# The recurrence's first chunk is started ahead of the solve, chunks 4 to 7 are prepared further back, and five buffers get other places

## The chip, the cores and the metric

One of the eight cores of a Trainium2 chip runs the whole program. The metric is the device time of one execution in microseconds (us). Engines: PE multiplies matrices, PEld loads its weights, ACT, DVE and POOL work element by element, SP issues DMA transfers.

## The reference, cut to what matters

A linear-attention recurrence over 768 steps for 4 x 8 heads of width 40 gives 3072 tokens of width 320; two feed-forward blocks follow.

```python
for t in range(S):                                   # S = 768
    y[:, :, t] = einsum('bhd,bhde->bhe', rt, state)
    Sa = einsum('bhde,bhe->bhd', state, at)
    state = state * wt[..., None, :] - einsum('bhd,bhe->bhde', Sa, bt) + einsum('bhd,bhe->bhde', vt, kt)
x = y.transpose(0, 2, 1, 3).reshape(B * S, H * D)
a, b = x @ w1, x @ w2
x = (a * b @ w3) @ w_out                             # 320 -> 1024 -> 1024 -> 320
h = maximum(x @ w_in, 0.0)
out = h * h @ w_out2                                 # 320 -> 2048 -> 320
```

The weights of the blocks come as 64-bit numbers.

## The kernel before

The recurrence goes by 24 chunks of 32 steps. Within a chunk it is a triangular system, and a chunk is worked off in stages, in this order: `do_x0` (right side of the system: 32 small products of `XL` with `RX`, the state), `do_sa` (times the inverse `TT`), `do_sat` (four transposes of the result `SA`, with copies by ACT into `vs` and `YI`), `do_l` (products of `vs` and `RT`, masked by DVE into `YI`, line 797), from chunk 1 on `do_z` (the old state transposed into `YR`), and `do_ys` (32 products; DVE makes the new state `RX` of them, line 828, and the output `yst`, line 832). The next chunk's `do_x0` needs that state.

Before a chunk can run it is prepared: `prep` loads its image `im` and decays `iw`, scans them on DVE (lines 570 to 580) and multiplies the image (chunks 0 to 3 on DVE, later ones on POOL, lines 592 and 598); `prep_pq` (written pq) makes 32 products, copied by ACT (`Pn`, line 615) and transposed by DVE (`qt`, line 618); `prep_kb` (kb) makes eight transposes of `im`, copied by ACT into `kn` (line 634). Each stores its result to DRAM through SP's queue, and the chunk's loads (`load_x` for `XL`, `load_rv` for `vs` and `RT`, `load_y`) read it back. `solve` inverts the systems of four chunks at once on DVE (lines 665 to 687: `PT` in, steps on `T`, `tt` out); for chunks 0 to 3 it does two halves, and `corner` joins them with two rounds of products on PE (lines 706 and 709).

Between the stages PE works from a list `fill`: first 64 `step`s that fold w3 and w_out into one matrix (line 472, written pw; in the trace two matmuls each), for which ACT (lines 332 to 335) and DVE (line 337) decode 64-bit weights in `raw` and `early` buffers into `wst`; then the token tiles of the first block (`ab`, line 380). The gaps after the stages say how much is pulled.

The order on PE is the order of the code; the other engines' and SP's orders come from a scheduler with priorities. Every engine and SP's queue work strictly in order. SP has at most eight transfers under way: each waits for the eighth before it. Products of the attention go through two PSUM buffers, `pat`, in turn: each stage waits until the one two places before it has been read out. Most other tiles have one buffer, too (`im` and `iw` for chunks 4 and 6 on, `suf`, `kn`, `qt`).

Of the kernel before, what the change touches and what calls it, by code (L numbers as in the profile page):

```python
# [17 lines left out]
C = 32  # L18
# [13 lines left out]
    ("solve", 0), ("kb", 1), ("kb", 2), ("kb", 3), ("prep", 4), ("pq", 4), ("kb", 4),  # L32
)
BETWEEN = {
    (0, "start"): (("prep", 5), ("prep", 6)),
    (0, "x0"): (("corner", 0),),
    (0, "sat"): (("w3",), ("corner", 1, 0)),
    (0, "l"): (("pq", 5), ("corner", 1, 1)),
    (0, "ys"): (("kb", 5), ("pq", 6), ("kb", 6)),
    (1, "start"): (("prep", 7),),  # L40
    (1, "sat"): (("corner", 2, 0),),
    (1, "l"): (("corner", 2, 1),),
    (1, "ys"): (("pq", 7), ("kb", 7), ("solve", 1)),
    (2, "start"): (("prep", 8),),
# [201 lines left out]
def body(tc, img, rv, rd, vn, vp, raw, w1, w2, w3t, wo, win, wo2, ident, maskt, out, dbg=None):  # L246
# [4 lines left out]
    with (  # L251
# [12 lines left out]
        with right, tc.manual_schedule(engines={mybir.EngineType.PE}):  # L264
# [240 lines left out]
            with (  # L505
# [61 lines left out]
                def prep_scan(c):  # L567
                    w_ = pr["w", c][0:104]
                    suf = first(c, "suf", [128, 529], {1: (at, "wt"), 3: (at, "wt")})
                    dve.tensor_tensor_scan(  # L570
                        out=suf[0:104, ::-1], data0=w_[:, ::-1], data1=mark[0:104, ::-1],
                        initial=0.0, op0=ALU.mult, op1=ALU.add)
                    whole = suf[0:104, 1::33]
                    g = gc[0:104, c % 8]

                    dve.scalar_tensor_tensor(out=g, in0=whole[:, 0:16], scalar=LEAST ** C, in1=whole[:, 0:16],
                                             op0=ALU.is_lt, op1=ALU.max)
                    dve.reciprocal(out=inv[0:104, ::33], in_=g)
# [23 lines left out]
                def prep_pq(c, cc):  # L602
# [11 lines left out]
                    qt = first(c, "qt", [128, 2, HZ, C], {1: (at, "yst"), 3: (at, "yst"), 6: (ma, "xr")})  # L614
# [8 lines left out]
                def prep_kb(c):  # L623
# [3 lines left out]
                    kn = first(c, "kn", [128, 2, HZ, 2, D], {1: (at, "rt"), 3: (at, "vs"), 6: (wa, "w1r")})  # L627
# [158 lines left out]
                def do_l(c):  # L786
# [98 lines left out]
                run(OPENING)  # L885
                solved = marks[0]
                YI = at.tile([128, NU, 72], F32, name="YI")
                RT = at.tile([128, 2, 16, C], F32, name="RT", tag="rt")
                XL = at.tile([128, 2, 16, C], F32, name="XL", tag="XL")
                for t in (XL[32:64], XL[96:128], YI[32:64], SA, RT):  # L890
                    nc.any.memset(t, 0.0)
                dve.tensor_copy(out=YI[0:D, :, C:72], in_=idt[0:D, 0:D].unsqueeze(1).to_broadcast([D, NU, D]))
                with tc.issue_after(ld.ins):
                    folds, more_w3 = fold(solved)
                    stage(load_x, 0)
                    stage(load_rv, 0)
                    stage(load_y, 0)
                fill.push(*folds)

                for c in range(NCH):  # L900
# [8 lines left out]
                    stage(do_x0, c, gap=gaps[0])  # L909
# [250 lines left out]
```

## Time and profile before

| | |
|---|---|
| median of 3 runs | 1065.53 us (1065.2 to 1065.82) |
| the profiled execution, its own time | 1073.37 us |
| its span, first to last instruction | 1071.6 us |
| PE busy | 920.5 us (86% of the span) |
| DVE busy | 693.1 us (65%) |
| ACT busy | 475.1 us (44%) |
| POOL busy | 224.0 us (21%) |

Shares of the whole span mix stages with different limits: PE is busy in 38 of the first 100 us and in 92.5 of the 104 us from 195.7 on.

### The profile page before, as it was taken

The numbers are of one execution on the slowest core, as the hardware profiler recorded it, in microseconds if no ns is written. First come the engines' busy times: TensorE is split into PE (matmuls) and PEld (weight loads), VectorE is DVE, ScalarE is ACT, GpSimd is POOL, SyncE is SP. The second block draws the span as 40 slices with busy tenths as digits, with TensorE's granted clock in tenths as the row PEclk, the third lists the DMA queues.
The fourth block names the chain that finished last, engine by engine and source line by source line (L and its number), as shares of the span: only waits on it lengthen the run. The fifth ranks groups of instructions, "written<-read, shape, count | busy, mean of one in ns | idle before, by whom it ended". The sixth has DMA issues, their size and how long they took to land.

```text
span 1071.6 us, 29226 instructions
## 1 busy us (share of the span) xinstructions
PE 920.5 (86%) x12240; PEld 824.2 (77%) x12240; DVE 693.1 (65%) x1366; ACT 475.1 (44%) x975; POOL 224.0 (21%) x304
## 2 busy tenths in 40 slices
PE   1337676899989889879899989889999999999997
PEld 1235554788879788778898889868998898898986
DVE  8753689568966985897489344887456554444432
ACT  2755776443343334433343433775333333333332
POOL 0332025433334443323200000552000000000000
PEclk9999787899999999989899989989999999999999
DMA  8977775676567667666645532665122121000001
GB/s 239 301 221 224 204 204 150 169 182 161 147 153 184 159 153 183 169 155 159 162 118 113 127 94 62 171 184 113 30 62 54 57 49 25 1 25 1 19 7 27
DMA packets 209389, 134.44 MB, mean 125 GB/s; under 512 B 143793, under 2 KB 184114, under 8 KB 209252
## 3 DMA queue, kind: packets, MB, share of 16 engines
q1 hardware_dynamic: 201892, 110.61, 40.6%
q0 software_dynamic: 7072, 21.57, 7.2%
q8 instruction: 98, 1.61, 0.7%
q10 hardware_dynamic: 288, 0.33, 0.1%
q14 instruction: 39, 0.32, 0.1%
HBM read 99.27 MB, written 33.19 MB: 124 GB/s over the span
## 4 chain that ended last, share of the span: by engine, by line
PE 52%; DVE 22%; DMA 12%; ACT 7%; issue 4%; SPq 2%; POOL 1%; ACTq 0%; DVEq 0%; POOLq 0%
PE ph L380 16%; PE po L1020 16%; PE ab L380 8%; PE px L438 4%; DVE T L675 3%; DVE tmp L672 3%; DMA im<-img 2%; PE pat L820 2%; DVE RX L828 2%; DMA early<-w 2%; DVE yst L832 2%; PE pat L792 2%; DVE suf L570 1%; DVE gl L418 1%; DVE wst L337 1%
## 5 line engine op out<-in xcount | busy, mean ns | idle before, releaser
L1020 PE MATMUL po<-wul,rh 128*128 128x320 f32 x384 | 118.3, 308 | 0.0
L1020 PE MATMUL po<-wuh,rh 128*128 128x320 f32 x384 | 118.0, 308 | 0.0
L1020 PE MATMUL po<-wuh,rl 128*128 128x320 f32 x384 | 116.9, 308 | 0.8 <-DVE rl L1007 0.8
L417 ACT CAST gh<-g 128x256 fp32r<-128x256 f32 x96 | 38.9, 405 | 99.2 <-DVE g L412 86.2
L380 PE MATMUL ph<-xh,wih 128*128 128x512 f32 x192 | 76.0, 396 | 0.7 <-POOL wil L351 0.7
L380 PE MATMUL ph<-xh,wil 128*128 128x512 f32 x192 | 75.7, 394 | 0.0
L380 PE MATMUL ph<-xl,wih 128*128 128x512 f32 x192 | 75.6, 394 | 0.0
L820 PE MATMUL pat<-YI,YR 128*40 128x72 f32 (+1 forms) x1536 | 60.8, 244 | 17.0 <-DVE qt L618 15.2
L1020 PEld LDWEIGHTS po<-wul,rh 128*128 128x128 f32 x384 | 72.0, 188 | 4.2
L411 ACT COPY a_sb<-ab 128x256 f32<-128x256 f32 x96 | 35.6, 371 | 89.1 <-PE ab L380 88.6
L1020 PEld LDWEIGHTS po<-wuh,rh 128*128 128x128 f32 x384 | 72.0, 188 | 3.8
L820 PEld LDWEIGHTS pat<-YI,YR 128*40 128x40 f32 x1536 | 55.9, 130 | 22.6 <-DVE qt L618 17.1
L1020 PEld LDWEIGHTS po<-wuh,rl 128*128 128x128 f32 x384 | 71.6, 188 | 1.3 <-DVE rl L1007 1.3
L438 PE MATMUL px<-wph,gh 128*128 128x320 f32 x192 | 66.6, 347 | 6.0 <-ACT gh L417 3.7
L675 DVE TENSOR_TENSOR T<-T,tmp 128x31 f32<-128x31 f32 (+20 forms) x170 | 66.2, 389 | 3.3
L672 DVE TENSOR_TENSOR tmp<-PT,T 128x31 f32<-128x31 f32 (+20 forms) x170 | 63.7, 375 | 3.6
L418 DVE TENSOR_TENSOR gl<-g,gh 128x256 fp32r<-128x256 f32 x96 | 45.9, 478 | 29.7 <-ACT gh L417 29.4
L438 PE MATMUL px<-wph,gl 128*128 128x320 f32 x192 | 61.5, 320 | 3.4 <-DVE gl L418 3.3
L380 PE MATMUL ab<-xh,w1h 128*128 128x256 f32 x192 | 58.0, 302 | 7.4 <-issue 4.0
L438 PE MATMUL px<-wpl,gh 128*128 128x320 f32 x192 | 61.0, 318 | 0.0
L412 DVE TENSOR_TENSOR g<-a_sb,ab 128x256 f32<-128x256 f32 x96 | 40.0, 416 | 31.2 <-ACT a_sb L411 30.2
L380 PE MATMUL ph<-xq,wir 128*128 128x512 f32 x192 | 60.1, 394 | 0.0
(539 smaller groups left out, 2482.5 us busy)
## 6 DMA issues: line engine op xcount, KB each, us to landing
raw<-w3t SPq DMA_DIRECT2D x16, 512.0 KB
YR<-KB_d SPq DMA_DIRECT2D x48, 160.0 KB
im<-img POOLq DMA_DIRECT2D x28, 240.0 KB, 5.0
wt<-AW_d SPq DMA_DIRECT2D x24, 214.5 KB
raw<-wo SPq DMA_DIRECT2D x16, 320.0 KB
RX<-vp SPq DMA_DIRECT2D x24, 208.0 KB
vs<-rv SPq DMA_DIRECT2D x24, 208.0 KB
KB_d<-kn POOLq DMA_DIRECT2D x14, 320.0 KB, 5.6
```

What stands on the lines that cost most here:

```text
L380: mm(out=ps, lhsT=seq[i][0], rhs=seq[i][1], start=(i == 0), stop=(i == 7))
L411: act.copy(out=a_sb, in_=ps[:, 0])
L412: dve.tensor_tensor(out=g, in0=a_sb, in1=ps[:, 1], op=ALU.mult)
L417: act.copy(out=t["gh"][:, ff], in_=g)
L418: dve.tensor_tensor(out=t["gl"][:, ff], in0=g, in1=t["gh"][:, ff], op=ALU.subtract)
L438: mm(out=ps, lhsT=a_, rhs=b_, start=(k == 0 and i == 0), stop=(k == 7 and i == 2))
L672: dve.tensor_tensor(out=tv, in0=Pv[:, :, s, s + 1:n].unsqueeze(3).to_broadcast(sh), in1=Tv[:, :, s, 0:s + 1].unsqueeze(2).to_broadcast(sh) ...
L675: return dve.tensor_tensor(out=o, in0=o, in1=tv, op=ALU.subtract).ins
L792: mm(out=ps[q:q + 64, 0, 32 * i - q // 2:32 * i - q // 2 + 64], lhsT=vs[0:104, i], rhs=RT[0:104, :, i], start=True, stop=True, tile_positi ...
L820: mm(out=ps[64 * y:64 * y + D, b, 72 * z:72 * z + n], lhsT=YR[:, u], rhs=YI[:, u, 0:n], start=True, stop=True, tile_position=(0, 64 * y))
L828: dve.tensor_tensor(out=o, in0=v[r, :, :, C:72], in1=decay.unsqueeze(3).to_broadcast([D, 2, HZ, D]), op=ALU.mult)
L1020: mm(out=po[j][g], lhsT=a_, rhs=b_, start=(ff == 0 and i == 0), stop=(ff == 15 and i == 2))
```

## The change

`do_x0` of chunk 0 and its loads stand behind the opening's last pq, ahead of the solve and of the kb of chunks 1 to 3; the rest of the opening becomes `SECOND_PART`. Pq and kb of chunks 4 to 7 stand further back among the stages. `wi` and `qt` of chunk 3, `kn` of chunks 1 and 4 and the small `x1` of `corner` get other places, away from those of `XL`, `yst`, `RT`, the common `kn` and `x2`. DVE's decode of later weights is ordered behind `do_l` of chunk 0 (`hold`). No operation is added or removed.

```diff
 OPENING = (
     ("prep", 0), ("prep", 1), ("prep", 2), ("prep", 3), ("pq", 0), ("kb", 0), ("pq", 1), ("pq", 2), ("pq", 3),
-    ("solve", 0), ("kb", 1), ("kb", 2), ("kb", 3), ("prep", 4), ("pq", 4), ("kb", 4),
 )
+SECOND_PART = (("solve", 0), ("kb", 1), ("kb", 2), ("kb", 3), ("prep", 4))
 BETWEEN = {
-    (0, "ys"): (("kb", 5), ("pq", 6), ("kb", 6)),
+    (0, "ys"): (("kb", 5),),
-    (1, "ys"): (("pq", 7), ("kb", 7), ("solve", 1)),
-    (2, "start"): (("prep", 8),),
+    (2, "x0"): (("pq", 7), ("kb", 7), ("solve", 1), ("prep", 8)),
...
-                    wi = first(c, "wi", [128, 528], {1: (at, "vs"), 2: (at, "rt"), 3: (at, "XL"), 6: (wa, "w2r")})
+                    wi = first(c, "wi", [128, 528], {1: (at, "vs"), 2: (at, "rt"), 3: (wa, "w2r"), 6: (wa, "w2r")})
...
-                    qt = first(c, "qt", [128, 2, HZ, C], {1: (at, "yst"), 3: (at, "yst"), 6: (ma, "xr")})
+                    qt = first(c, "qt", [128, 2, HZ, C], {1: (at, "yst"), 3: (ma, "xr"), 6: (ma, "xr")})
...
-                    kn = first(c, "kn", [128, 2, HZ, 2, D], {1: (at, "rt"), 3: (at, "vs"), 6: (wa, "w1r")})
+                    kn = first(c, "kn", [128, 2, HZ, 2, D], {1: (ma, "x2"), 3: (at, "vs"), 4: (wa, "w1r"), 6: (wa, "w1r")})
...
-                        TT["x1"] = ma.tile([128, H, 16], F32, name="x1", tag="x2")
+                        TT["x1"] = ma.tile([128, H, 16], F32, name="x1", tag="xf")
...
+                    if c == 0:
+                        hold.append(o.ins)
...
                 run(OPENING)
+                XL = at.tile([128, 2, 16, C], F32, name="XL", tag="XL")
+                for t in (XL[32:64], XL[96:128]):
+                    nc.any.memset(t, 0.0)
+                with tc.issue_after(ld.ins):
+                    stage(load_x, 0)
+                stage(do_x0, 0)
+                run(SECOND_PART)
...
-                    stage(do_x0, c, gap=gaps[0])
+                    if c:
+                        stage(do_x0, c, gap=gaps[0])
```

On PE, from the last pq of the opening on (`im_109`, `im_114`, `im_117` are the images of chunks 1 to 3, `im_105` that of chunk 4, line 758 is `do_x0`, 768 `do_sa`, 775 `do_sat`), there stood before:

```order
L611 MATMUL pat_302<-im_117 32x64 x32
L630 MATMUL pat_400<-idt_63,im_109 128x104 x8
L630 MATMUL pat_413<-idt_63,im_114 128x104 x8
L630 MATMUL pat_426<-idt_63,im_117 128x104 x8
L611 MATMUL pat_458<-im_105 32x64 x32
L630 MATMUL pat_496<-idt_63,im_105 128x104 x8
L758 MATMUL pat_634<-RX_97,XL_511 32x40 x32
L706 MATMUL pat_674<-tt_342,early_103 32x16 x32
L709 MATMUL pat_708<-x1_673,early_103 16x16 x32
L768 MATMUL pat_745<-X0_101,tt_342 32x40 x32
L775 MATMUL pat_779<-idt_63,SA_102 104x128 x4
```

and there stands now:

```order
L611 MATMUL pat_302<-im_117 32x64 x32
L758 MATMUL pat_348<-RX_97,XL_340 32x40 x32
L630 MATMUL pat_442<-idt_63,im_109 128x104 x8
L630 MATMUL pat_455<-idt_63,im_114 128x104 x8
L630 MATMUL pat_468<-idt_63,im_117 128x104 x8
L706 MATMUL pat_606<-tt_384,early_103 32x16 x32
L709 MATMUL pat_640<-x1_605,early_103 16x16 x32
L768 MATMUL pat_677<-X0_101,tt_384 32x40 x32
L611 MATMUL pat_711<-im_105 32x64 x32
L775 MATMUL pat_749<-idt_63,SA_102 104x128 x4
L630 MATMUL pat_759<-idt_63,im_105 128x104 x8
```

`do_x0` moved ahead of three kb; pq and kb of chunk 4 moved behind `do_sa` and `do_sat`.

On DVE, ahead of the read-out of `do_ys` of chunk 0 (the two `RX` and two `yst` rows; `suf_1056` and `suf_1164` are the scan of chunk 7, `suf_774` that of chunk 6; line 797 is the masking of `do_l`, `qt_744` the transposition of pq of chunk 4, `qt_894` of chunk 5), there stood before:

```order
L570 SCALAR_TENSOR_TENSOR suf_1056<-iw_106,mark_93 104x529
L576 SCALAR_TENSOR_TENSOR gc_95<-suf_1056 104x16
L578 RECIPROCAL inv_94<-gc_95 104x16
L580 SCALAR_TENSOR_TENSOR wi_1060<-iw_106,inv_94 104x528
L337 SCALAR_TENSOR_TENSOR wst_789<-wst_789,raw_790 128x512
L797 TENSOR_TENSOR YI_509<-pat_838,msk_64 64x8x2x32 x2
L618 STREAM_TRANSPOSE qt_894<-pat_861 128x256
L828 TENSOR_TENSOR RX_97<-pat_937,gc_95 40x8x40 x2
L832 TENSOR_TENSOR yst_936<-pat_937,wt_599 40x2x4x32 x2
L828 TENSOR_TENSOR RX_97<-pat_958,gc_95 40x8x40 x2
```

and there stands now (lines 797, 828 and 832 are there 797, 830 and 834):

```order
L618 STREAM_TRANSPOSE qt_744<-pat_711 128x256
L797 TENSOR_TENSOR YI_500<-pat_824,msk_64 64x8x2x32 x2
L337 SCALAR_TENSOR_TENSOR wst_847<-wst_847,raw_848 128x512
L618 STREAM_TRANSPOSE qt_894<-pat_861 128x256
L570 SCALAR_TENSOR_TENSOR suf_1164<-iw_106,mark_93 104x529
L576 SCALAR_TENSOR_TENSOR gc_95<-suf_1164 104x16
L578 RECIPROCAL inv_94<-gc_95 104x16
L580 SCALAR_TENSOR_TENSOR wi_1168<-iw_106,inv_94 104x528
L830 TENSOR_TENSOR RX_97<-pat_937,gc_95 40x8x40 x2
L834 TENSOR_TENSOR yst_936<-pat_937,wt_582 40x2x4x32 x2
L830 TENSOR_TENSOR RX_97<-pat_958,gc_95 40x8x40 x2
L834 TENSOR_TENSOR yst_936<-pat_958,wt_582 40x2x4x32 x2
```

The scan of chunk 7 moved from ahead of the masking to between it and the read-out, and the transposition of pq of chunk 4 now stands directly ahead of the masking.

On ACT, around the read-out of `do_sa` of chunk 2 (the row `SA_102<-pat_1594`; `early_2103` holds two pieces of w1 and w2 as loaded, `raw_` such of w3), there stood before:

```order
L333 ACTIVATE early_2103<-early_2103 128x512
L335 ACTIVATE early_2103<-early_2103 128x512
L760 ACTIVATE X0_101<-pat_1543 128x320
L333 ACTIVATE raw_1632<-raw_1632 128x512
L332 ACTIVATE wst_1353<-raw_1354 128x512
L335 ACTIVATE raw_1632<-raw_1632 128x512
L333 ACTIVATE early_2103<-early_2103 128x512
L335 ACTIVATE early_2103<-early_2103 128x512
L770 COPY SA_102<-pat_1594 128x8x40
L474 CAST wph_70<-pw_1360 128x320
L332 ACTIVATE wst_1579<-raw_1580 128x512
L780 COPY YI_509<-SA_102 32x8x40 x4
```

and there stands now:

```order
L634 COPY kn_1459<-pat_1458 128x8x40 x2
L333 ACTIVATE raw_1632<-raw_1632 128x512
L335 ACTIVATE raw_1632<-raw_1632 128x512
L770 COPY SA_102<-pat_1594 128x8x40
L333 ACTIVATE raw_1654<-raw_1654 128x512
L474 CAST wph_70<-pw_1360 128x320
L332 ACTIVATE wst_1405<-raw_1406 128x512
L780 COPY YI_500<-SA_102 32x8x40 x4
L335 ACTIVATE raw_1654<-raw_1654 128x512
L333 ACTIVATE early_2103<-early_2103 128x512
L369 CAST xq_2240<-xr_2234 128x256
L777 COPY vs_1235<-pat_1642 104x4x4x32
```

The two pairs that decode `early_2103` moved behind the read-out; the first pair now stands ahead of the copy into `vs` (line 777), on which `do_l` waits.

## Rows read from the trace of the kernel before

A timeline's row gives the start in us, the duration in us, engine, line, operation, tiles, shapes and count, and in brackets the idle time before it with what ended it; a window's row gives its length, then busy time of PE, PEld, DVE, ACT and POOL with counts, PEclk, DMA share and GB/s.

**Rows 1.** Busy time by stage: window, its length, then the columns named above.
```profile
0.00:100.00 100.00, 38.03 (x1130) 31.20 (x1130) 64.41 (x130) 47.88 (x89) 23.32 (x32) 1.00 0.83 244
100.00:195.70 95.70, 70.12 (x1119) 50.51 (x1119) 72.23 (x137) 71.12 (x119) 33.89 (x33) 0.80 0.68 185
195.70:300.00 104.30, 92.54 (x1741) 86.21 (x1736) 79.71 (x180) 39.21 (x93) 38.77 (x59) 0.97 0.64 164
```

**Rows 2.** Timeline of PE, the opening and chunk 0.
```profile
49.56 1.65 PE L630 MATMUL pat<-idt,im 104*128 104x104 f32 x8 [0.65 <-ACT kn L634]
58.77 1.29 PE L758 MATMUL pat<-RX,XL 128*32 128x40 f32 x64 [7.57 <-ACT kn L634]
60.46 1.05 PE L706 MATMUL pat<-tt,early 32*32 32x16 f32 x64 [0.39 <-DVE qt L618]
...
63.00 1.85 PE L768 MATMUL pat<-X,tt 32*32 32x40 f32 x48 [0.37 <-ACT tt L717]
...
72.40 1.98 PE L792 MATMUL pat<-RT,vs 104*64 104x64 f32 x32 [1.29 <-DMA RT<-rv]
...
82.14 0.72 PE L709 MATMUL pat<-x,early 32*16 32x16 f32 x64 [4.64 <-DVE YI L797]
82.79 4.07 PE L820 MATMUL pat<-YI,YR 128*40 128x72 f32 x64
```

**Rows 3.** Timeline of PE, chunk 1 to the first token product.
```profile
93.49 0.80 PE L758 MATMUL pat<-RX,XL 128*32 128x40 f32 x64
...
101.57 1.10 PE L775 MATMUL pat<-idt,SA 128*104 128x128 f32 x4 [2.59 <-ACT SA L770]
...
106.06 1.15 PE L792 MATMUL pat<-RT,vs 104*64 104x64 f32 x32
...
129.21 1.44 PE L758 MATMUL pat<-RX,XL 128*32 128x40 f32 x64 [5.34 <-DVE qt L618]
...
143.70 1.10 PE L775 MATMUL pat<-idt,SA 128*104 128x128 f32 x4 [6.33 <-ACT SA L770]
...
195.69 0.39 PE L380 MATMUL ab<-xh,w1h 128*128 128x256 f32 x1
```

**Rows 4.** Timeline of DVE: the solve of chunks 0 to 3, and behind it.
```profile
34.80 0.29 DVE L675 TENSOR_TENSOR T<-T,tmp 128x126 f32<-128x126 f32 x1
...
40.10 0.45 DVE L618 STREAM_TRANSPOSE qt<-pat 128x256 f32<-128x256 f32 x1 [3.70 <-DMA Q_d<-qt]
40.48 0.70 DVE L675 TENSOR_TENSOR T<-T,tmp 128x128 f32<-128x128 f32 x1
...
51.49 1.04 DVE L684 STREAM_TRANSPOSE early<-T 128x256 f32<-128x256 f32 x2
...
76.93 1.26 DVE L570 TENSOR_TENSOR_SCAN suf<-iw,mark 104x529 f32<-104x529 f32 x1 [12.61 <-DMA iw<-img]
...
80.61 1.39 DVE L797 TENSOR_TENSOR YI<-pat,msk 64x512 f32<-64x512 f32 x2
...
84.99 0.99 DVE L828 TENSOR_TENSOR RX<-pat,gc 40x320 f32<-40x320 f32 x2 [2.51 <-PE pat L820]
...
129.08 1.14 DVE L665 STREAM_TRANSPOSE PT<-Pn 128x256 f32<-128x256 f32 x2
```

**Rows 5.** Timeline of POOL: products of the image of chunk 4.
```profile
40.34 2.92 POOL L598 TENSOR_TENSOR im<-im,suf 104x256 f32<-104x256 f32 x4
```

**Rows 6.** Timeline of ACT: three instructions that waited or were waited for.
```profile
57.92 0.75 ACT L634 COPY kn<-pat 128x320 f32<-128x320 f32 x2 [8.15 <-DMA KB_d<-kn]
...
141.33 0.67 ACT L333 ACTIVATE early<-early 128x512 uint32<-128x512 uint32 x1 [4.47 <-DMA early<-w]
...
143.13 0.52 ACT L770 COPY SA<-pat 128x320 f32<-128x320 f32 x1
```

**Rows 7.** Busy time in two stretches, columns as in the first group.
```profile
40.00:56.00 16.00, 7.45 (x96) 6.33 (x96) 14.67 (x35) 9.77 (x17) 10.23 (x13) 1.00 0.94 289
129.08:192.33 63.25, 47.61 (x697) 33.82 (x698) 56.93 (x113) 44.68 (x75) 24.02 (x23) 0.81 0.68 185
```

More of the change, by code (lines that the diff above doesn't have):

```diff
@@ L31 @@
     ("prep", 0), ("prep", 1), ("prep", 2), ("prep", 3), ("pq", 0), ("kb", 0), ("pq", 1), ("pq", 2), ("pq", 3),
-    ("solve", 0), ("kb", 1), ("kb", 2), ("kb", 3), ("prep", 4), ("pq", 4), ("kb", 4),
 )
+SECOND_PART = (("solve", 0), ("kb", 1), ("kb", 2), ("kb", 3), ("prep", 4))
 BETWEEN = {
-    (0, "start"): (("prep", 5), ("prep", 6)),
+    (0, "start"): (("prep", 5),),
     (0, "x0"): (("corner", 0),),
-    (0, "sat"): (("w3",), ("corner", 1, 0)),
-    (0, "l"): (("pq", 5), ("corner", 1, 1)),
-    (0, "ys"): (("kb", 5), ("pq", 6), ("kb", 6)),
-    (1, "start"): (("prep", 7),),
-    (1, "sat"): (("corner", 2, 0),),
+    (0, "sa"): (("pq", 4),),
+    (0, "sat"): (("kb", 4), ("prep", 6), ("corner", 1, 0)),
+    (0, "l"): (("w3",), ("pq", 5), ("corner", 1, 1)),
+    (0, "ys"): (("kb", 5),),
+    (1, "sa"): (("pq", 6),),
+    (1, "sat"): (("kb", 6), ("prep", 7), ("corner", 2, 0)),
     (1, "l"): (("corner", 2, 1),),
-    (1, "ys"): (("pq", 7), ("kb", 7), ("solve", 1)),
-    (2, "start"): (("prep", 8),),
+    (2, "x0"): (("pq", 7), ("kb", 7), ("solve", 1), ("prep", 8)),
     (2, "sat"): (("corner", 3, 0),),
@@ L796, in do_l @@
                         r = slice(64 * q, 64 * q + 64)
-                        dve.tensor_tensor(out=yl[:, q, :, :, 0:C],
+                        o = dve.tensor_tensor(out=yl[:, q, :, :, 0:C],
                                           in0=ps[r, 0].rearrange("p (i y t) -> p i y t", y=2, t=C),
                                           in1=msk[r].unsqueeze(1).unsqueeze(1).to_broadcast([64, 8, 2, C]), op=ALU.mult)
+                    if c == 0:
+                        hold.append(o.ins)
                 def do_z(c):
@@ L888, in body @@
                 RT = at.tile([128, 2, 16, C], F32, name="RT", tag="rt")
-                XL = at.tile([128, 2, 16, C], F32, name="XL", tag="XL")
-                for t in (XL[32:64], XL[96:128], YI[32:64], SA, RT):
+                for t in (YI[32:64], SA, RT):
                     nc.any.memset(t, 0.0)
@@ L894, in body @@
                     folds, more_w3 = fold(solved)
-                    stage(load_x, 0)
                     stage(load_rv, 0)
```

## The prediction, made before the changed kernel was run

> **What bounds the kernel now.** I read the busy times by stage first [rows 1]. PE is busy for 38.03 of the first 100 us, for 70.12 of the next 95.7 and for 92.54 of the 104.3 after that. So time that an order can give lies ahead of 195.69 us, where the first token product `ab` starts [rows 3]: 87.5 of these 195.7 us PE isn't busy. From there on PE's list is the same in both kernels and nearly full. I therefore count how much earlier the first `ab` comes, and take the end to move by as much.
>
> Next I read PE's timeline, stage by stage, for what ended each wait. In the opening [rows 2] `do_x0` of chunk 0 waits 7.57 us for a copy of kb of chunk 4, which itself waited 8.15 us for an older `kn` to be stored [rows 6]; the second corner of chunk 1 waits 4.64 us for DVE's masking. Later [rows 3] `do_sat` of chunks 1 and 2 waits 2.59 and 6.33 us for ACT's read-out of `SA`, `do_x0` of chunk 2 waits 5.34 us for a transposition of pq of chunk 7, which stands ahead of it. Then I read the engines that were waited for. On DVE [rows 4] the masking ran at 80.61, behind the scan of chunk 7 that had waited 12.61 us for `iw`. On ACT [rows 6] the read-out of `SA` of chunk 2 ran right behind a decode that had waited 4.47 us for weights. Last, two floors [rows 7]: between 40 and 56 us the DMA engines are 94% busy at 289 GB/s, and from the start of the second solve (129.08, rows 4) to its end at 192.33 DVE is busy for 56.93 of 63.25 us.
>
> **The change, part by part.** Nothing is removed or added, so each term is a wait that goes, comes or shrinks. I follow the chain of chunks and give at each point its lead, the time by which it comes earlier.
>
> *To the first corner.* What moves forward: 32 products, one ACT copy, five loads in SP's queue and two clearings of `XL`; behind them go three kb (24 transposes, six copies, three stores), and further back pq and kb of chunk 4 and chunk 5's image load. `XL` reads what pq of chunk 0 stored; that store landed at 40.1 [rows 4]. At most eight transfers are ahead of a load; at 0.2 to 0.3 MB each they are 2 MB, 7 us at 289 GB/s [rows 7], so I estimate `do_x0` at 48 (the ends are 41, and 58, when PE no longer waited for loads before). Then come 1.29 us for it, three kb at 1.65 [rows 2] and one copy of 0.75 [rows 6] between buffers: 55.0.
>
> The solve must be through by then, too. It ended at 52.53 [rows 4]. Its stall of 3.70 us for the same store now comes five steps sooner, so ten instructions of 0.29 us run behind it, against a scan of 1.26 and a transposition with its mask (about 0.9) that leave: 0.7 later, 53.3. POOL's products of chunk 4 now fall into the second half. Where they fell before, an instruction took 0.70 instead of 0.29 us [rows 4, 5]; over four products in 2.92 us that costs DVE 2.92 x (1 - 0.29/0.70) = 1.7 us at most: 55.0. So the corner starts at 55.0 and not at 60.46: lead 5.5. The ends are 7.2 (it starts with the solve's end at 53.3) and 0 (loads late).
>
> The Trainium skill (SBUF — State Buffer, Who interferes with whom) speaks against part of this lead: a DVE instruction with two SBUF inputs contends with a GpSimd instruction that reads SBUF, through a lock that blocks the loser fully. By that the whole 2.92 us would be lost, the solve would end at 56.2 and the lead be 4.3, the final sum 1.2 us smaller. The 0.70 of the row says that it isn't blocked for the whole of a product of 0.73 (2.92 / 4), though, and I stay with the row.
>
> *To `do_ys` of chunk 0.* Before, corner to `do_ys` took 22.3 us (60.46 to 82.79). Now pq and kb of chunk 4 lie between. The masking loses its 12.61 us wait, but a new chain comes: kb 4 needs pq 4 transposed, on DVE behind chunk 6's scan; that needs POOL's products of chunk 5 (one `suf`), whose image can load only when kb of chunk 1 is through (51). Image 51 to 57, two scans and small work 3 (1.26 each), POOL 3 to 4, scan 3, kb 1.65, corner 1.05, `do_l` 1.98, masking 1.39: 73. Behind `do_l` come pq 5 and a corner, whose copies stand on ACT behind decodes, for which I add 4: `do_ys` at 77, lead 5.8. The ends are 73 (lead 9.8) and 82.8 (lead 0).
>
> *To `do_x0` of chunk 1.* Before, 10.7 us (82.79 to 93.49), with kb 5, pq 6 and kb 6 between. Now kb 5 alone is there; but on DVE chunk 7's scan stands ahead of the read-out. It waits for POOL's products of chunk 6, whose image loads when kb 4 is through (68): 75, POOL 79, scan 82, and the four pairs of read-out 3.5 (0.99 for two, rows 4): 85.5, lead 8. The end below is 0, if that image lands 8 us later.
>
> *To `do_x0` of chunk 2.* pq 6 and kb 6 now lie in here, under PE's waits; the 2.59 us ahead of `do_sat` goes. `do_l` still waits for weights: the copy of kb 6 on ACT stands behind a decode of w1, whose loads come at most a few us sooner. I take 100 for `do_l` against 106.06. Behind it the wait of 5.34 goes, with pq 7 and kb 7 (about 0.9 each), which stand behind `do_x0` now: lead 6 + 7.1 = 13, `do_x0` at 116. The ends are 7.1 (chunk 1 gains nothing) and 15.
>
> *To the first `ab`.* Pq 7 follows `do_x0` and five pw; so the second solve starts near 121.5 instead of 129.08, lead 7.5. The read-out of `SA` of chunk 2 no longer stands behind the 4.47 us wait; the decode that waited stands ahead of the copy into `vs` instead, and `do_l` of chunk 2 waits for it if its weights are late. Up to here the lead is 13, but DVE has the same work from the solve's start to its end, so the solve ends at 121.5 + 63.25 = 184.8 if its idle time stays (6.3 us), and at 178.4 if all of it goes. DVE's queue holds decodes of w3 between the steps; their transfers don't come sooner by the whole lead, so I expect a few more us of waiting there. The lead that arrives at `ab` I take as 6: the solve's 7.5 less 1.5. Its ends are 2 (6 us of new waits on DVE) and 13 (DVE doesn't hold PE up).
>
> *Priced at nothing.* The clearings of `XL` at the start of DVE and ACT lie ahead of first transfers (at most 1.26, a scan). Chunk 4's `iw` loads behind six loads of w_out, and its scan ahead of chunk 3's last product can start the solve late; the stall of 3.70 covers that much, and a wait like the 12.61 would cost 8.9. The five places: `kn` of chunk 4 loses the wait of 8.15, and `RT` can be loaded early, which takes the 1.29 us ahead of `do_l` [rows 2]; `x1` in `xf` delays only the first tile's load, needed at `ab`, 190. The order behind `hold` costs nothing while the masking comes before the weights.
>
> **Sum.** Leads: 5.5 at the corner, 5.8 at `do_ys`, 8 at chunk 1, 13 at chunk 2, 6 at `ab`. The profiled execution took 1073.37 us, so it becomes 1067.4. The runs have a median of 1065.53, 7.8 below it; by the same 6 us I forecast 1059.5.
>
> **The rivals.**
> - The whole lead arrives. For it: DVE is idle for 36 of the first 100 us [rows 1], so the read-outs may be early enough. Against it: 90% busy behind 129. Time: 1065.5 - 12 = 1053.5.
> - The transfers bind, so the loads of chunks 0 and 1 don't come sooner whatever the order: 94% busy [rows 7], and the bytes are the same. The first lead shrinks to 1 and the later ones to what pq 7 gives, of which DVE's queue takes most. Time: 1064.5, no change that could be measured. It is also the case that the change doesn't do what it says: the loads, not the copies, held `do_x0`.
> - Slower: one place, DVE's read-out of `do_ys` of chunk 0 behind chunk 7's scan. Two image loads, five POOL products twice and two scans stand in a row there, with one buffer each. It decides when chunk 6's image lands later than about 83 (I expect 75); each further us delays every later chunk. Landing at 86, it gives 1068.5. Against it: the same kind of scan waited until 76.93 before with the queue as full.
>
> **How the numbers follow.** Part of the lead (gains from 2.2 to 10 us): 0.60. Whole lead (over 10): 0.12. Transfers bind: 0.14. Slower: 0.14, of which 0.02 lies within 0.2%. Two runs of this kernel can be told apart from about 0.2%, 2.1 us. Faster: 0.72; within: 0.16; slower: 0.12. The likeliest case alone spans 1055.5 to 1063.3. The range of 8 in 10 takes in the transfers' case and part of both outer ones: 1053.5 to 1067.0.
>
> **What would show it.** `do_x0` of chunk 0 near 48 and the corner near 55; chunk 7's scan on DVE ending near 82 and `do_x0` of chunk 1 near 85; `do_x0` of chunk 2 near 116 with no wait for a transposition; the second solve starting near 121.5; the first `ab` near 189.7. The forecast is wrong if chunk 6's image lands late, if the loads of `XL` arrive after 52, if DVE's decodes hold the second solve, or if the stretch behind the first `ab` isn't equally long.

## The result and the profile after

The changed kernel takes 1074.64 us (median of 20 runs, 1068.52 to 1079.10), the kernel before 1066.09 (20 runs, 1061.47 to 1072.01): a ratio of 1.0073, 95% interval 1.0055 to 1.0091 (of the two medians alone it is 1.0080). It is slower; forecast was 1059.5, in a range of 1053.5 to 1067.0.

The profiled execution took 1071.37 us, with a span of 1069.5. That is 2.0 us *less* than the profiled execution of before, though the medians differ by 8.6 us the other way: it lies 3.3 us below its own median, and that of before 7.3 us above its own. Single profiles show here where things wait, but their difference isn't the result. I therefore took a second profile of both (r1 below). Busy time by stage, columns as in [rows 1]:

```profile
0.00:100.00 100.00, 37.84 (x1057) 31.05 (x1058) 63.95 (x129) 49.59 (x90) 19.17 (x30) 0.83 0.82 233
100.00:195.70 95.70, 70.41 (x1211) 51.19 (x1211) 70.03 (x127) 70.69 (x121) 34.83 (x33) 0.86 0.68 197
195.70:300.00 104.30, 92.62 (x1728) 85.53 (x1727) 85.05 (x196) 38.70 (x92) 41.06 (x63) 0.97 0.67 167
```

PE isn't busy for 87.5 of the first 195.7 us, within 0.1 us as before. The granted clock of the first 100 us reads 0.83 and not 1.00, but up to 80 us the same products take as long in both kernels (a kb 1.65 us, `do_l` 1.98), so I read no cause from that column; only at 93.97, behind a wait of 5.82 us, `do_x0` takes 1.29 us and not 0.80. PE's timeline, the places of [rows 2, 3]:

```profile
47.99 1.33 PE L758 MATMUL pat<-RX,XL 128*32 128x40 f32 x64 [16.95 <-DMA RT<-rv]
...
53.60 0.85 PE L706 MATMUL pat<-tt,early 32*32 32x16 f32 x64
...
68.48 1.65 PE L630 MATMUL pat<-idt,im 104*128 104x104 f32 x8 [3.10 <-DVE qt L618]
...
75.42 1.98 PE L792 MATMUL pat<-RT,vs 104*64 104x64 f32 x32 [4.31 <-DMA vs<-rv]
...
80.43 0.94 PE L822 MATMUL pat<-YI,YR 128*40 128x72 f32 x11 [0.74 <-DVE qt L618]
...
92.13 1.62 PE L630 MATMUL pat<-idt,im 104*128 104x104 f32 x8 [5.82 <-DVE yst L834]
93.97 1.29 PE L758 MATMUL pat<-RX,XL 128*32 128x40 f32 x64 [0.23 <-PE pat L630]
...
111.27 1.98 PE L792 MATMUL pat<-RT,vs 104*64 104x64 f32 x32 [3.07 <-ACT kn L634]
...
127.02 0.80 PE L758 MATMUL pat<-RX,XL 128*32 128x40 f32 x64
...
193.59 0.39 PE L380 MATMUL ab<-xh,w1h 128*128 128x256 f32 x1
```

`do_x0` of chunk 0 comes at 47.99 (58.77 before), the corner at 53.60 (60.46): 6.9 us of lead. At `do_ys` of chunk 0 it is 2.4, at `do_x0` of chunk 1 it is gone (93.97 against 93.49), `do_l` of chunk 1 is 5.2 late, and the first `ab` comes at 193.59 (195.69). In between, `do_l` of chunk 0 waits 4.31 us for `vs`, and kb of chunk 5 waits 5.82 us for DVE's read-out of `do_ys`. DVE's timeline at that place (answers to [rows 4]):

```profile
86.66 1.76 DVE L570 TENSOR_TENSOR_SCAN suf<-iw,mark 104x529 f32<-104x529 f32 x1 [6.29 <-POOL im L598]
...
88.97 1.26 DVE L580 TENSOR_TENSOR_SCAN wi<-iw,inv 104x528 f32<-104x528 f32 x1
90.14 0.96 DVE L830 TENSOR_TENSOR RX<-pat,gc 40x320 f32<-40x320 f32 x2
```

The read-out (lines 830 and 834) could run near 82.6, 2.2 us behind the start of the products (84.99 against 82.79 in [rows 4, 2]), and ran at 90.14: the scan of chunk 7 ahead of it waited until 86.66 and ended only then. It waited for POOL's products of chunk 6, and these for their image. POOL's timeline:

```profile
82.89 1.18 POOL L592 TENSOR_TENSOR im<-im,wi 104x512 f32<-104x512 f32 x1 [13.67 <-DMA im<-img]
```

and that of SP's queue (issues; the duration is the time that the queue stood there):

```profile
67.68 0.43 SPq L743 DMA_DIRECT2D vs<-rv  x1
68.17 5.65 SPq L600 DMA_DIRECT2D AW_d<-im  x1
...
75.52 0.72 SPq L550 DMA_DIRECT2D im<-img  x2
```

The image's buffer was free when kb of chunk 4 was through, at 70.1 (the row at 68.48). But the queue stood at a store for 5.65 us, for what these rows don't show, so the load was issued at 75.52 and POOL began at 82.89.

The second solve (of chunks 4 to 7), too, comes later. DVE's timeline, its first row and its last transposition:

```profile
132.78 2.11 DVE L665 STREAM_TRANSPOSE PT<-Pn 128x256 f32<-128x256 f32 x4
...
199.53 0.63 DVE L678 STREAM_TRANSPOSE tt<-T 128x256 f32<-128x256 f32 x1
```

It goes from 132.78 to 200.16, where before it went from 129.08 to 192.33: the first `ab` now comes ahead of the solve's end.

A second place lies far behind the edit, between the two blocks. PE's timeline at the first products `ph` of the second block, of the changed kernel:

```profile
706.50 0.31 PE L438 MATMUL px<-wph,gl 128*128 128x320 f32 x1
710.63 0.76 PE L380 MATMUL ph<-xh,wih 128*128 128x512 f32 x1 [3.82 <-POOL wul L974]
711.19 0.63 PE L380 MATMUL ph<-xl,wih 128*128 128x512 f32 x1
```

and of the kernel before:

```profile
713.71 0.31 PE L438 MATMUL px<-wph,gl 128*128 128x320 f32 x1
714.67 0.47 PE L380 MATMUL ph<-xh,wih 128*128 128x512 f32 x1 [0.66 <-POOL wil L351]
714.98 0.40 PE L380 MATMUL ph<-xl,wih 128*128 128x512 f32 x1
```

PE waits 3.82 us where it waited 0.66. The row names POOL. DVE's timeline tells more, of the changed kernel

```profile
708.09 0.48 DVE L337 SCALAR_TENSOR_TENSOR wst<-wst,raw 128x320 uint32<-128x320 uint32 x1
708.60 0.49 DVE L340 SCALAR_TENSOR_TENSOR wst<-raw,wst 128x320 uint32<-128x320 uint32 x1
709.01 1.09 DVE L337 SCALAR_TENSOR_TENSOR wst<-wst,raw 128x256 uint32<-128x256 uint32 x1
710.03 0.50 DVE L443 STREAM_TRANSPOSE x<-px 128x320 f32<-128x320 f32 x1
```

and of the kernel before:

```profile
712.30 0.78 DVE L337 SCALAR_TENSOR_TENSOR wst<-wst,raw 128x256 uint32<-128x256 uint32 x1 [0.23 <-ACT wst L332]
714.06 0.52 DVE L443 STREAM_TRANSPOSE x<-px 128x320 f32<-128x320 f32 x1 [0.97 <-PE px L438]
```

Line 443 reads the last product of the first block, `px`, out of PSUM; lines 337 and 340 decode weights. Before, DVE has come to the read-out and waits 0.97 us for the product; now six more decodes stand ahead of it (15 in a row, and not 9). In both, `ph` starts 0.1 us behind its end (710.53 and 710.63; 714.58 and 714.67). And the first `ph` then take 0.63 us each, where they took 0.39 to 0.40: in their first 3 us the granted clock is 0.50 (1.2 GHz) in the changed kernel and 1.00 (2.4 GHz) in that of before. Busy time from 710.6 on in the changed kernel:

```profile
710.60:713.60 3.00, 2.97 (x7) 2.42 (x8) 2.93 (x6) 1.94 (x5) 1.98 (x3) 0.50 0.74 244
```

and from 714.6 on before:

```profile
714.60:717.60 3.00, 2.93 (x13) 2.47 (x14) 2.93 (x5) 1.74 (x5) 1.88 (x2) 1.00 0.65 186
```

### The profile page after: what moved, and what is told of

Read it like the earlier page. It is cut to its first block, busy times and chain, and to the rows that moved or that the text cites. A ratio compares the mean times of both kernels' runs of the same rounds, so it can differ in the third digit from the quotient of the medians.

```text
span 1069.5 us, 29217 instructions
## 1 busy us (share of the span) xinstructions
PE 921.4 (86%) x12240; PEld 824.7 (77%) x12240; DVE 694.6 (65%) x1366; ACT 476.8 (45%) x976; POOL 223.5 (21%) x303
## 4 chain that ended last, share of the span: by engine, by line
PE 50%; DVE 23%; DMA 12%; ACT 6%; issue 4%; SPq 3%; POOL 1%; ACTq 0%; POOLq 0%; DVEq 0%
PE ph L380 17%; PE po L1028 16%; PE ab L380 7%; DVE tmp L672 4%; DVE T L675 4%; PE px L438 3%; DMA im<-img 3%; DMA raw<-w3t 2%; DVE RX L830 2%; PE pat L822 2%; DVE yst L834 2%; DMA X_d<-yst 2%; DVE g L412 1%; DVE wst L337 1%; DVE gl L418 1%
## 5 line engine op out<-in xcount | busy, mean ns | idle before, releaser
L411 ACT COPY a_sb<-ab 128x256 f32<-128x256 f32 x96 | 35.6, 371 | 85.5 <-PE ab L380 85.0
L672 DVE TENSOR_TENSOR tmp<-PT,T 128x31 f32<-128x31 f32 (+20 forms) x170 | 68.7, 404 | 3.5
L598 POOL TENSOR_TENSOR im<-im,suf 104x256 f32<-104x256 f32 x80 | 59.2, 768 | 5.2 <-DMA im<-img 5.2
```

The lines of the kernel that those rows point to most:

```text
L411: act.copy(out=a_sb, in_=ps[:, 0])
L598: eng.tensor_tensor(out=kb[:, g, :, :, j], in0=kb[:, g, :, :, j], in1=sg, op=ALU.mult)
L672: dve.tensor_tensor(out=tv, in0=Pv[:, :, s, s + 1:n].unsqueeze(3).to_broadcast(sh), in1=Tv[:, :, s, 0:s + 1].unsqueeze(2).to_broadcast(sh) ...
```

## Experiments

All ratios are to runs of the kernel before on the same chip. "x0(1)" is the start of `do_x0` of chunk 1, "`ab`" that of the first token product, "idle" PE's wait ahead of the first `ph`, all in us, from one profile each.

| run | edit | ratio, 95% interval | x0(1) | `ab` | idle |
|---|---|---|---|---|---|
| r1_before | none | 1.0006, 0.9977 to 1.0034 | 93.5 | 193.2 | 0.66 |
| r1_after | the change | 1.0079, 1.0048 to 1.0110 | 95.3 | 196.4 | 4.21 |
| e1 | the five places alone | 1.0030, 1.0004 to 1.0056 | 93.9 | 191.2 | 3.91 |
| e2 | the order alone | 1.0085, 1.0052 to 1.0117 | 95.6 | 201.8 | 0.66 |
| e3 | change, `kn`(1) back | 1.0069, 1.0035 to 1.0103 | 94.9 | 194.3 | 0.66 |
| e4 | change, scan 7 held | 0.9991, 0.9972 to 1.0011 | 87.6 | 187.0 | 0.66 |
| e5 | four places, not `x1` | 1.0010, 0.9982 to 1.0039 | 93.0 | 190.2 | 0.66 |
| e6 | `kn`(1) alone | 1.0070, 1.0043 to 1.0097 | 96.6 | 194.4 | 4.81 |
| e7 | change, decodes held | 1.0030, 1.0006 to 1.0053 | 93.9 | 194.1 | 0.65 |
| e8 | both held | 0.9988, 0.9963 to 1.0012 | 86.3 | 185.9 | 0.66 |
| e9 | front half alone | 1.0025, 0.9997 to 1.0052 | 97.5 | 195.1 | 0.66 |
| e10 | back half alone | 1.0022, 0.9996 to 1.0049 | 92.7 | 195.3 | 0.66 |
| e11 | before, less DVE work | 1.0039, 1.0011 to 1.0067 | 92.3 | 191.5 | 0.66 |
| e12 | e8, less DVE work | 1.0016, 0.9990 to 1.0042 | 92.1 | 190.9 | 0.66 |

**Both kernels again.** No edit.

> The kernel before, unchanged, for a second profile and to see how far single executions lie apart: the profiled execution of before (1073.37 us) lies 7.3 us above the median of its 20 runs, that of the changed kernel (1071.37) 3.3 us below its own. Theory A (the order of the stages costs the time) expects the first token product again near 195.7 us and a span near 1064 us, with the time between that product and the end 869 us and not 876. Theory B (the buffer places cost it) expects the same of this run. Both expect a ratio of 1.00 within 0.002.

> The changed kernel again, for a second profile: a ratio of 1.005 to 1.009 by either theory. Theory A expects the loss ahead of the first token product: that product no longer 2.1 us sooner than before (193.59) but later than 197. Theory B expects it behind that product: 193 to 195 us there, and the stretch behind it longer than before's by 5 us or more.

The ratio came again. Both single theories failed: the first `ab` lies at 193.2 and 195.7 in the two profiles of before, at 193.6 and 196.4 in those of the changed kernel, so little is lost up to there. The stretch from it to the last `px` took 513.5 and 518.0 before, 512.9 and 517.8 after: it scatters by 5 us in either kernel. What differs in every pair is the idle time ahead of `ph`; of the two runs below, e1 (places) has it and e2 (order) hasn't.

**Places alone (e1) and order alone (e2).** e1 is the kernel before with these lines, e2 the changed kernel without them:

```diff
-  wi   {1: (at, "vs"), 2: (at, "rt"), 3: (at, "XL"), 6: (wa, "w2r")}
+  wi   {1: (at, "vs"), 2: (at, "rt"), 3: (wa, "w2r"), 6: (wa, "w2r")}
-  qt   3: (at, "yst")
+  qt   3: (ma, "xr")
-  kn   {1: (at, "rt"), 3: (at, "vs"), 6: (wa, "w1r")}
+  kn   {1: (ma, "x2"), 3: (at, "vs"), 4: (wa, "w1r"), 6: (wa, "w1r")}
-  x1   tag="x2"
+  x1   tag="xf"
```

> The kernel before with nothing but the five other places (`wi` and `qt` of chunk 3, `kn` of chunks 1 and 4, `x1`). The order of the code is that of before. Theory B expects most of the loss here: a ratio of 1.005 or more. Theory A expects 0.996 to 1.001: the places only take waits away (7.57 us of PE's wait ahead of the right side of chunk 0 hangs on `kn` of chunk 4).

> The changed kernel with the five buffers back in the places of before. Theory A expects a ratio of 1.006 or more, since the order is that of the changed kernel and the old places only add waits. Theory B expects 0.995 to 1.002, without the loss.

e1 lies between what the two theories expected of it; e2 fits A. But each loses in another place: e1 is 2 to 4.5 us early at `ab` and waits at `ph`; e2 is 6 to 9 us late at `ab` and doesn't wait at `ph`. That points to two losses. Neither run is a clean half, though: the scheduler answers each with another order. In the traces DVE's order differs from that of before at some 80 places in e1, the first at 3 us, and from that of the change at some 60 in e2.

**The read-out between the blocks (e3, e5, e6, e7).** In the traces 15 decode rows stand ahead of the read-out in the changed kernel, e1 and e6, and 9 in before, e2, e3, e5 and also in e4, e9 and e10, which keep all five places. So `kn` of chunk 1 in the place of `x2` is enough in the kernel before, and putting it back is enough in the change, but other edits move the read-out as well. Up to 703 us DVE's order is the same in the change, e3 and e7; in e3 ACT's differs at five places between 106 and 113 us.

```diff
 e3 (on the change), reversed in e6 (on before)
-  kn   {1: (ma, "x2"), ...
+  kn   {1: (at, "rt"), ...
 e7 (on the change): line 443
-  dve.transpose(out=x2..., in_=ps...)
+  o = dve.transpose(out=x2..., in_=ps...)
+  if (n, g) == (11, 1):
+      hold.append(o.ins)          # decodes issued from here on stand behind it
```

> The changed kernel with one buffer put back, `kn` of chunk 1 in the place of `RT`. On DVE the order ahead of the second block is that of the changed kernel row for row; only behind it the read-out of the last block-one product (line 443) stands behind 9 decode rows as before, and not behind 15. Theory C (two separate losses, one of them the second block's first products, which wait 4.1 to 4.5 us for that read-out and then run at a lower clock) expects the wait at about 1 us, the first product token as in the changed kernel (193.5 to 196.5) and 4 to 5 us less: a ratio of 1.003 to 1.0045. Theory A (all of the loss is the order of the opening) expects the ratio of the changed kernel, 1.007 to 1.009.

> The kernel before with four of the five places (all but `x1`), with 9 decode rows ahead of the last read-out, as before. The version with all five took 1.003 with a wait of 4.2 us at the second block and a first token product at 191.2. Theory C expects that wait at about 1 us and the first token product at 190 to 194: a ratio of 0.997 to 1.000. Theory B (the places themselves cost time in the opening) expects 1.002 or more.

> The kernel before with nothing but `kn` of chunk 1 in the place of `x2`. This alone puts the last read-out behind 15 decode rows. Theory C expects the second block's first product to wait about 4.2 us and the ratio at 1.003 to 1.005, with the first token product as before (193 to 196). If the wait behind that row is hidden, the ratio is 0.999 to 1.001.

> The changed kernel, all places as changed, with the later decodes of the second block's weights held on DVE behind the read-out of the last block-one product: it then stands behind 6 decode rows, and not behind 15. The order ahead of it is that of the changed kernel. Putting back `kn` of chunk 1 had brought only 1.0069 against 1.0079, with an interval of 0.0034 to either side, though its profile showed the wait of 4.2 us gone. Theory C (the wait and the low clock behind it cost what the profile shows, 4 to 5 us) expects the second block's first product to wait at most 1 us and 1.002 to 1.0045. Theory F (what is gained there is taken back, by decodes that now come late for the second block's products) expects 1.006 to 1.008 and new waits of 3 us or more behind the first of these products.

e6, one buffer's place and nothing else, is 1.0070 (its runs lie at 1070.36 to 1076.74), even more than C expected; its interval reaches down to 1.0043. It doesn't price the read-out alone: from 133 us on DVE's order differs from that of before at 60 places, and `do_x0` of chunk 1 already comes 3 us late. PE's row:

```profile
712.80 0.69 PE L380 MATMUL ph<-xh,wih 128*128 128x512 f32 x1 [4.81 <-POOL wul L966]
```

e7 takes the wait away and leaves the order of every engine as in the change up to 703 us, the cleanest of these runs; PE's timeline:

```profile
711.15 0.47 PE L380 MATMUL ph<-xh,wih 128*128 128x512 f32 x1 [0.65 <-issue]
711.46 0.40 PE L380 MATMUL ph<-xl,wih 128*128 128x512 f32 x1
```

and DVE's:

```profile
710.53 0.52 DVE L443 STREAM_TRANSPOSE x<-px 128x320 f32<-128x320 f32 x1 [3.54 <-PE px L438]
```

It is 1.0030, 0.0043 or 4.6 us below the change's 1.0073, within what theory C expected from the profiles: 3.82 - 0.66 = 3.2 us of wait, and from the start of the first `ph` to that of the last `po` (first and last starts of these tiles) 350.2 and 349.8 us, against 348.9 and 348.2 before, 1.4 more, which goes with the low clock behind the wait. That both sums give 4.6 is luck: the two ratios leave 1.4 to 7.8 us. Theory F fell: no new wait appeared. e3 hit its profile (idle 0.66) but not its time: 1.0069, with runs from 1065.26 to 1079.32 and an interval that still holds the upper half of what C expected. e5 (e1 without `x1`, its read-out behind 9 rows) points the same way, 1.0010 against e1's 1.0030, but within each other's intervals, and just above C's 0.997 to 1.000.

**The scan of chunk 7 (e4, e8).**

```diff
 e4 and e8: prep_scan
-  dve.tensor_tensor_scan(out=suf..., data0=w_..., data1=mark...)
+  with tc.issue_after(out0[-1]) if c == 7 else nullcontext():   # out0: the yst rows of do_ys
+      dve.tensor_tensor_scan(out=suf..., data0=w_..., data1=mark...)
 e8 also: the hold of e7
```

> The changed kernel with the scan of chunk 7 ordered on DVE behind the read-out of chunk 0's last products (in the changed kernel it stands ahead, waits until 86.66 us and ends at 90.14). The read-out of the last block-one product stands behind 9 decode rows here, so the 4 to 5 us of theory C are given back as well. Theory D (this scan loses the lead of the opening, the slower rival of the prediction) expects the read-out at once behind the products, near 81 to 85 us, the right side of chunk 1 at 85 to 88 and not at 94 to 95, and the first token product at 188 to 190: a ratio of 0.994 to 0.998. Theory E (a later wait takes the lead anyway: the copy of kb of chunk 6 on ACT behind a decode, or DVE from the second solve on) expects the right side of chunk 1 as early, but the first token product at 193 to 196 and a ratio of 1.002 to 1.005.

> Both: the scan of chunk 7 behind the read-out of chunk 0, and the later decodes behind the last read-out. The scan alone (with 9 decode rows ahead of the last read-out) took 0.9991, with the first token product at 187.0. Theory D (the scan loses the opening's lead) expects 187 to 189 again and a ratio of 0.996 to 0.9995. If the gain of the scan was chance, the ratio is 1.002 or more.

DVE in e8, where the read-out (line 833) now stands ahead of the scan (line 573):

```profile
82.47 0.99 DVE L833 TENSOR_TENSOR RX<-pat,gc 40x320 f32<-40x320 f32 x2 [2.25 <-PE pat L825]
...
86.25 1.64 DVE L573 TENSOR_TENSOR_SCAN suf<-iw,mark 104x529 f32<-104x529 f32 x1
```

and PE at the two places that follow:

```profile
86.32 0.84 PE L761 MATMUL pat<-RX,XL 128*32 128x40 f32 x64 [0.49 <-PE pat L633]
...
185.87 0.39 PE L380 MATMUL ab<-xh,w1h 128*128 128x256 f32 x1
```

The lead at chunk 1 stays: `do_x0` at 86.32 (the prediction had 85.5), the first `ab` at 185.9, 7.3 us ahead of r1_before. Up to this scan the order of all engines in e8 is that of e7, so theory D is right that the scan loses the opening's lead. The ratio falls by 0.0042 or 4.5 us against e7, and by 0.0078 from e3 to e4, which differ in the place of `kn` of chunk 1, too; that is the scan's place together with what the scheduler made of it, since behind it DVE's order differs at 36 places up to 184 us. E expected `ab` at 193 to 196 and fell. But e4's 0.994 to 0.998 was missed, and 0.9991 and 0.9988 are no gain over the kernel before that can be told.

**The halves (e9, e10).**

```diff
 e9 (on the change): BETWEEN as before, no hold in do_l
-SECOND_PART = (("solve", 0), ("kb", 1), ("kb", 2), ("kb", 3), ("prep", 4))
+SECOND_PART = (("solve", 0), ("kb", 1), ("kb", 2), ("kb", 3), ("prep", 4), ("pq", 4), ("kb", 4))
 e10 (on the change)
-                stage(do_x0, 0)
                 run(SECOND_PART)
+                stage(do_x0, 0)
```

> The front half of the change alone: the right side of chunk 0 directly behind the opening's products, the five places as changed, but pq and kb of chunks 4 to 7 and the decodes where they stood before. 9 decode rows stand ahead of the last read-out. Theory D (the loss is chunk 7's scan, whose image comes late only where pq and kb of chunks 4 to 7 go back) expects the right side of chunk 0 near 48 us, but the corner, which stands behind kb of chunk 4, not sooner than 58, the right side of chunk 1 at 91 to 94, the first token product at 190 to 193, as with the places alone, and a ratio of 0.997 to 1.001. If the early right side itself costs the time (its loads pushed ahead of others), 1.004 or more.

> The back half alone: pq and kb of chunks 4 to 7 where the change puts them, the places as changed, but the right side of chunk 0 behind the solve and kb of chunks 1 to 3. 9 decode rows stand ahead of the last read-out; the scan of chunk 7 still stands ahead of the read-out of chunk 0. Theory D expects the loss here: the scan ends near 90, the right side of chunk 1 at 93 to 96, the first token product at 193 to 196 and a ratio of 1.002 to 1.006. If both halves are needed for the loss, 0.999 or less.

Neither half is faster; both lie near 1.002, on the edge of what can be told from no change. e9 was not as theory D had it: `do_x0` of chunk 0 stands at 48.1, but x0(1) and `ab` come later than expected, since `do_l` of chunk 0 waits longer for its loads than in any other run (PE's timeline):

```profile
79.58 1.97 PE L792 MATMUL pat<-RT,vs 104*64 104x64 f32 x32 [11.46 <-DMA vs<-rv]
```

So the early right side may have a price of its own, since other loads stand behind its five; this is argued, not shown. e10 lies near D's numbers (`ab` 195.3; x0(1), at 92.7, a little sooner), but not for D's reason. Its scan of chunk 7 ended at 88.56, and DVE's read-out then still waited for PE's products:

```profile
88.83 0.99 DVE L830 TENSOR_TENSOR RX<-pat,gc 40x320 f32<-40x320 f32 x2 [0.27 <-PE pat L822]
```

So the scan takes nothing there: `do_ys` of chunk 0 came at 86.6, and not at 80.4, and with it there was no lead left to lose.

**Where e8's lead goes (e11, e12).** Both leave out the low bits of w3, so their results aren't the reference's.

```diff
 e11 (on before), e12 (on e8); the hold of e7 in both: fetch
-    dve.scalar_tensor_tensor(out=ou, in0=ou, scalar=3, in1=lo, ...)
+    if (K, N) != (4, 128):
+        dve.scalar_tensor_tensor(out=ou, in0=ou, scalar=3, in1=lo, ...)
```

> The kernel before without the 16 instructions by which DVE joins the low bits to the decoded w3 (128x512, 0.67 to 0.83 us each, some 12 us of DVE's work ahead of the first token product), and with the later decodes held behind the last read-out. It leaves out the low bits of w3, so its result is not the reference's. It is the control for the run beside it. Both theories expect it a little sooner than before: the first token product at 186 to 192, a ratio of 0.993 to 0.998.

> The changed kernel with the scan of chunk 7 and the later decodes held, as in the version that took 0.9988, and without the same 16 instructions of DVE (the low bits of w3 are left out here too). Theory G (DVE's queue between the second solve and the fourth chunk takes the lead of the opening) expects the lead to come through now: the first token product 6 to 8 us ahead of the control's, the products of chunk 4 at least 5 us ahead, and a ratio 0.004 to 0.007 below the control's. Theory H (PE's own list behind that product, or the transfers, limit the stretch) expects the same small difference as with the full work: 0.000 to 0.002 below the control's, the products of chunk 4 at most 3 us ahead.

Inconclusive. With 16 rows fewer the scheduler set DVE's opening anew, and e12 lost its lead before the place that it was to test: `do_ys` of chunk 0 waited 7.03 us for a transposition, x0(1) came at 92.1 and `ab` at 190.9, beside the control's 92.3 and 191.5. Neither theory is borne out by it. The control itself got slower (1.0039) with some 12 us less of DVE's work, though its first `ab` came 1.7 us ahead of r1_before's; DVE's order differs from that of before at some 85 places, and what of it costs the time isn't shown.

## Why the prediction was wrong

**To the corner: right.** `do_x0` at 47.99 (48 forecast), the corner at 53.60 (55.0). The solve ended at 52.8, where I had 53.3 to 55.0. A step of it took 0.61 us beside POOL's products, where a larger one without them took 0.29 ([rows 4]); DVE's timeline:

```profile
45.27 1.12 DVE L672 TENSOR_TENSOR tmp<-PT,T 128x96 f32<-128x96 f32 x1
...
47.09 0.61 DVE L672 TENSOR_TENSOR tmp<-PT,T 128x78 f32<-128x78 f32 x1
...
51.73 1.07 DVE L684 STREAM_TRANSPOSE early<-T 128x256 f32<-128x256 f32 x2
```

and POOL's:

```profile
45.07 1.21 POOL L592 TENSOR_TENSOR im<-im,wi 104x512 f32<-104x512 f32 x1 [6.59 <-DMA iw<-img]
46.24 2.67 POOL L598 TENSOR_TENSOR im<-im,suf 104x256 f32<-104x256 f32 x4
```

By the Trainium skill (SBUF — State Buffer, Who interferes with whom) the loser of that port is blocked fully. The trace agrees for one instruction at a time: five of DVE's steps ended there, each 0.07 to 0.12 us behind the end of one of POOL's five, the first after 1.12 us beside a product of 1.21. But a step came through with each product of 0.67 us, so the whole of POOL's time isn't lost, and the solve didn't end at 56.2, the prediction's sum for that. My reason against the page, that a step of 0.70 can't have been blocked for a whole product, doesn't hold; that the loss stays below the whole time does.

**To `do_ys` of chunk 0: mis-sized.** 80.43 and not 77: `vs` was issued at 67.68 and held `do_l` for 4.31 us. I had counted the early `RT` as a gain, and not asked when `vs` would come in a queue that had grown.

**To `do_x0` of chunk 1: here the first step failed.** "Whose image loads when kb 4 is through (68): 75, POOL 79, scan 82". Kb 4 was through at 70.1, but SP's queue stood 5.65 us at a store, and a load that I put at 7 us from the buffer's release took 7.4 from an issue at 75.52. The chain ended at 90.2 and not at 82. The place, the mechanism and the point from which it decides (a landing later than about 83; it was 82.89, and 84.17 in r1_after) were those of the slower rival, which had a chance of 0.14 and a time of 1068.5. Without the second loss the change is near that, e7 with 1.0030 or 1065.53 x 1.0030 = 1068.7, but by luck: 1068.5 was for a landing at 86, and in e7 (landing at 82.8, `ab` at 194.1, no wait at `ph`) the profile shows no place for its 3.2 us, of which the interval leaves 0.6 to 5.6.

**To the second solve: mis-sized, the scan aside.** Forecast were `do_x0` of chunk 2 at 116 and a solve from 121.5 to 184.8. In e8, which keeps the lead, `do_x0` of chunk 2 came at 118.9, and DVE's timeline has the solve's first row and its last transposition at:

```profile
127.64 2.08 DVE L668 STREAM_TRANSPOSE PT<-Pn 128x256 f32<-128x256 f32 x4
...
192.49 0.64 DVE L681 STREAM_TRANSPOSE tt<-T 128x256 f32<-128x256 f32 x1
```

So of 10.3 us of lead at chunk 2, 1.4 are left at the solve's start and none at its end (193.13; 192.33 before). Pq 7, which stood ahead of `do_x0` of chunk 2, now stands behind it and five pw: from `do_x0` to the solve it takes 8.7 us in e8 and 5.8 in the change, where I had 5.5. And the solve takes 65.5 and 67.4 us, against 63.25 before; there I had allowed for a few more.

**From the first `ab` on: the second step failed.** "From there on PE's list is the same in both kernels ... take the end to move by as much". I had compared PE's list there; PE and ACT differ in a few rows near the second block's start, and DVE's order differs there in the place of one read-out, with 15 decode rows ahead of it instead of 9. That costs some 4.6 us (e7; 1.4 to 7.8). None of the rivals had it. It doesn't need the early chunk: in the kernel before the place of one small buffer brings it about (e6), through the scheduler. And the end doesn't follow the first `ab`: e8's came 7.3 to 9.8 us sooner than before, more than the 6 forecast, for a gain of 1.3 us (-1.3 to 3.9); in e5, e11 and e12, none with the wait at `ph`, it came at 190.2 to 191.5, and none is faster than before.

**The sum.** 1.0073 = 0.9988 (e8) + 0.0042 (the scan) + 0.0043 (the read-out). Each of the two differences has the uncertainty of two intervals of 0.0018 to 0.0024; e3 and e4 split it otherwise, 0.0078 for the scan and 0.0004 for the read-out, and e6 alone would give 0.0070 for the read-out. So the shares are known less well than the places.

**What stays open: why 7 us of lead at `ab` bring nothing.** Even without both losses the end doesn't move by as much as `ab`. In e8 the lead on r1_before is 7.3 at the first `ab`, 5.9 at `do_ys` of chunk 3, 4.4 at chunk 4, 1.1 at chunk 10; on the first profile of before it is 9.8, 8.4, 7.8 and 5.9 at the same places, so that up to 5 us of this hang on which execution it is held against. Busy time ahead of `ab` and just behind it, columns as in [rows 1], of r1_before:

```profile
175.00:187.00 12.00, 8.93 (x168) 6.11 (x170) 11.65 (x22) 6.37 (x13) 6.65 (x6) 0.86 0.51 147
187.00:200.00 13.00, 13.00 (x211) 10.89 (x208) 7.73 (x20) 6.88 (x13) 5.89 (x8) 1.00 0.54 133
```

and of e8:

```profile
175.00:187.00 12.00, 11.16 (x143) 8.12 (x144) 11.63 (x22) 8.81 (x16) 5.10 (x6) 0.86 0.34 79
187.00:200.00 13.00, 10.07 (x241) 9.17 (x240) 11.45 (x28) 3.44 (x10) 4.76 (x8) 1.00 0.75 202
```

Before, PE is full there and DVE busy for 7.73 of 13 us; in e8 DVE is busy for 11.45 and PE for 10.07. Up to that point DVE is full in both (11.65 and 11.63 of 12). So the work that DVE had not done when `ab` came early it does behind it (the solve ends at 193.13, 7 us behind the first `ab`; in r1_before it ended 1.9 ahead of it), and PE waits. That the solve keeps no lead is shown; that this is why the end keeps none, theory G, is argued and not shown: the runs that were to test it lost their lead earlier. That part of the lead is only lost in the scatter of the later stretch can't be excluded either.

## What to carry to other kernels

Where a scheduler orders the queues, compare the order of *every* engine over the *whole* program before you say that a stretch stays the same: here an edit at the start moved one read-out some 500 us further on, for some 4.6 us. The same holds for every control: one buffer put elsewhere moved DVE's order at 60 places, and of the runs here only e7 beside the change, and e8 beside e7, left every engine's order alone up to the place in question. A row that stands first in an engine's queue costs what its slowest input costs, so ask for each such row whose load is behind it, and price that load from the queue's rows, with the time that the queue stands. And where executions scatter by 10 us, take two profiles of each kernel before reading a difference of 2 us into them.

## What the runs showed of the hardware

- A short wait cost more than its length: behind 3.82 us of idle time the first `ph` took 0.63 us each, with the granted clock at its lower level, where behind 0.66 us they took 0.39. From the first `ph` to the last `po` that made 1.4 us against the mean of the two profiles of before; in e6, behind 4.81 us, 0.7.
- The row's releaser (POOL, line 974) was not the one that counted: in every profile of this case `ph` starts 0.1 us behind the end of DVE's read-out, whichever row is named.
- DVE's steps with two SBUF inputs and POOL's products went in step: one step ended with each product, 0.6 us a step where one alone took 0.29 or less, and POOL's four products took 2.67 us beside them and 2.60 alone.
- Executions of one program lay 10.5 us apart (1061.47 to 1072.01) on 20 runs, and the stretch behind the first `ab` took 513 or 518 us in the same kernel.
